# Other slots for the loads, splits and turns of q and k in a fused attention and MLP kernel

## The chip, the cores and the metric

The kernel runs on one core of one Trainium2 chip. The metric is the device time of one execution in microseconds (us). Before the change three executions took 505.07, 507.79 and 510.07 us, so the median is 507.79 us. One more execution was profiled.

Engines: PE multiplies matrices (PEld is its weight load), DVE is the vector engine, ACT the scalar engine, POOL is GpSimd, and SP is the sync engine, which here only issues DMAs.

## The reference, cut to what matters

```python
# q, k, v: (8 batches, 8 heads, 576 positions, 64), float32; w_in (512, 2048), w_out (2048, 512)
scores = scale * np.matmul(q, k.transpose(0, 1, 3, 2))
thresh = np.max(scores, axis=-1, keepdims=True) - tau        # tau = 0.02
scores = np.where(scores >= thresh, scores, -1000000000.0)
attn = softmax(scores)
attn_out = np.matmul(attn, v)
x = attn_out.transpose(0, 2, 1, 3).reshape(8 * 576, 512)
h = x @ w_in
out = (h - np.tanh(h)) @ w_out
```

An attention that keeps only scores within tau of the row's maximum is followed by a two-layer MLP over the 4608 tokens.

## The kernel before, in words

**Tiles.** Two heads of one batch form a pair; there are 32 pairs (NPAIR), and each has nine tiles of 128 query rows (TPP = 9), so 288 tiles in all. A tile's chain is: scores on PE (L387, matmuls L401 and L410), scaling and row maximum on DVE into sc (L420), a shift by maximum and tau on DVE (L432), the threshold on ACT into z (L447), the transpose of z into zT, exp on ACT into pT (L483, or L475 where PE made the transpose), and the product with v on PE (L506 to L524). From pair 6 on, zT is made by a DMA transpose on SP's queue, one for two tiles (L454).

**Preparing a pair.** k and q are loaded as float32 (kraw, qraw), split on POOL into a float16 high and low part (khl, qhl; three instructions, L228, L231, L232), and turned, so that the head dimension lies across partitions (kT, qT). In pairs 0 to 7 PE turns q, in pairs 0 to 8 it turns k; after that `turn` issues a DMA transpose on SP's queue (L315). A swapped copy of kT, kS, is made on POOL (`swap`, L337, two copies), after kT is there: the scores of a tile use kT and kS. v is copied to bf16 on POOL (`split_v`, L261 to L266). From pair 8 on, loads are issued by ACT's queue (`load_part`, L175) in up to two parts for each tensor. Raw tiles and split tiles have two buffers for each tensor (`raw_pool`, `hl_pool`), kT, qT and kS three each (`qk_pool`).

**Order.** The schedule is written out by hand: a loop over slots s, from -8 on (L852). In slot s the program emits, in this order, the shift of tile s + 7, the scores of tile s + 8, the threshold of tile s + 5 with its zT transpose when that tile is odd (so at even slots), tanh of the MLP, exp of tile s (from pair 6 on), MLP matmuls and their store, attention of tile s - 2, and last the planned steps of the slot (`plan`, L899). Each engine works through its own instructions in that order and waits only for semaphores; so a slot is a place in each queue and no fixed time.

**The plan.** The first scores of pair p stand in slot 9p - 8. A step with the number d stands d slots earlier, at 9p - 8 - d. The names in the table `LATER` (even pairs under 0, odd ones under 1) and in `FIRST_LATER` (pairs 8 and 9, which begin the scheme) are: k0, q0, q1, v0, v1 for the loads' parts; ks, qs, vs for splits; kt, qt for turns; kw for the swap. The loop at L784 puts them into `plan`. The parts are 288 KB for k, 256 and 32 KB for q, 160 and 128 KB for v.

Beside this, from pair 4 on, the MLP's matmuls are spread over the slots of four pairs at a time (hidden layer psH L579, second layer psY L605, a store of 256 KB for each 128 rows, L620), and after the last tile the rest of the MLP runs alone.

Of the kernel before, what the change touches and what calls it, by code (L numbers as in the profile page):

```python
# [18 lines left out]
def kernel(  # L19
# [713 lines left out]
    def w_load(piece):  # L733
# [6 lines left out]
        else:  # L740
# [18 lines left out]

    LATER = {  # L760
        0: (
            ("kt", 11), ("qt", 7), ("k0", 18), ("q0", 17), ("v0", 13),
            ("q1", 14), ("v1", 10), ("ks", 12), ("qs", 8), ("vs", 4),
            ("kw", 6),
        ),
        1: (
            ("kt", 10), ("qt", 6), ("k0", 18), ("q0", 14), ("v0", 15),
            ("q1", 13), ("v1", 12), ("ks", 11), ("qs", 8), ("vs", 6),
            ("kw", 5),
        ),  # L770
    }
    FIRST_LATER = {
# [3 lines left out]
            ("kw", 3),  # L776
        ),
        9: (
            ("kt", 10), ("qt", 6), ("k0", 18), ("q0", 14), ("v0", 15),
            ("q1", 13), ("v1", 12), ("ks", 11), ("qs", 8), ("vs", 6),  # L780
            ("kw", 5),
        ),
    }
    for p in range(DUAL, NPAIR):  # L784
# [176 lines left out]
```

## Time and profile before

| what | value |
|---|---|
| three executions, median | 507.79 us |
| the profiled execution | 511.62 us |
| its span | 509.7 us |
| PE busy | 484.8 us, 95% of the span |
| ACT busy | 431.7 us, 85% |
| DVE busy | 400.2 us, 79% |
| POOL busy | 291.4 us, 57% |
| DMA transposes zT, kT, qT | 117, 23, 24 |
| median from issue to landing: zT, kT, qT | 4.7, 5.2, 4.3 us |
| longest from issue to landing: zT, kT, qT | 9.8, 8.8, 6.3 us |

The profile is one execution. Busy time counts an engine's instructions; an instruction that only waits or issues a DMA is not counted. A queue name with a q, such as SPq or ACTq, is the issuing side of that engine. A line of waits has the form "who waited <- for whom: us in total, times, longest". A releaser is inferred from semaphores. The span splits in two: to about 440 us attention and MLP run together, and after that the remaining MLP runs alone. The granted TensorE clock was 0.57 on average between 104 and 108 us and full in the stretches around it.

### The profile page before, as it was taken

What the parts mean: (1) busy time and instruction counts of PE and PEld (TensorE: products, weight loads), DVE (VectorE), ACT (ScalarE), POOL (GpSimd) and SP (SyncE); (2) the same over time, 40 slices, a digit from 0 to 9 for tenths busy, and PEclk for the clock granted to TensorE, in tenths of its full rate; (3) what the DMA queues carried; (4) which work ended last, traced back from release to release, by engine and by line L of the source; (5) the groups of instructions that cost most, each with busy time, mean ns of one, the idle gap of its engine ahead of it and who ended that gap; (6) DMA issues with size and microseconds to landing.
All of it is one profiled execution on the core that took longest, in us unless ns stands there. A gap on an engine that the chain in (4) does not pass through costs nothing.

```text
span 509.7 us, 12184 instructions
## 1 busy us (share of the span) xinstructions
PE 484.8 (95%) x4283; PEld 270.9 (53%) x4345; DVE 400.2 (79%) x1150; ACT 431.7 (85%) x617; POOL 291.4 (57%) x390
## 2 busy tenths in 40 slices
PE   8999899889999989999999999999998999999997
PEld 4666566445555545555555555555554555544444
DVE  5899978878889879988898789889886887544440
ACT  5999998889999889999999999899979999533430
POOL 8999999886765375757675666569456700000000
PEclk9999999989999999999999999999999999999999
DMA  7852658999999999999999999999999986311013
GB/s 206 262 155 89 195 190 220 159 225 214 231 217 245 192 254 209 238 241 242 242 195 221 261 238 225 207 242 240 213 191 258 187 144 115 87 41 42 23 41 82
DMA packets 233341, 95.32 MB, mean 187 GB/s; under 512 B 203968, under 2 KB 222656, under 8 KB 233280
## 3 DMA queue, kind: packets, MB, share of 16 engines
q1 hardware_dynamic: 212336, 72.87, 75.1%
q10 hardware_dynamic: 20944, 21.67, 16.1%
q8 instruction: 34, 0.56, 0.5%
q14 instruction: 27, 0.22, 0.2%
HBM read 36.70 MB, written 9.44 MB: 91 GB/s over the span
## 4 chain that ended last, share of the span: by engine, by line
PE 57%; POOL 12%; DMA 9%; issue 7%; ACT 7%; DVE 5%; ACTq 1%; SPq 0%; POOLq 0%; DVEq 0%
PE psY L605 18%; PE psH L579 14%; PE psS L410 13%; DMA zT<-z 6%; PE psO L513 3%; POOL kS L337 3%; PE psHt L579 3%; ACT pT L483 3%; DMA vraw<-in_v_dram 3%; ACT z L447 2%; DVE g L598 2%; POOL qhl L232 2%; DVE sc L420 2%; PE psS L401 2%; ACTq L175 1%
## 5 line engine op out<-in xcount | busy, mean ns | idle before, releaser
L420 DVE TENSOR_SCALAR_CACHE_REDUCE sc<-psS 128x576 f32<-128x576 f32 x288 | 213.5, 752 | 27.1 <-PE psS L410 12.9
L447 ACT ACTIVATE z<-sc,nb 128x576 bf16<-128x576 f32 x288 | 216.1, 770 | 8.0 <-DVE nb L432 5.7
L483 ACT ACTIVATE pT<-zT 128x1152 f16<-128x1152 bf16 x117 | 135.2, 1155 | 12.3 <-DMA zT<-z 10.6
L605 PE MATMUL psY<-w_out_sb,g 128*128 128x512 bf16 (+1 forms) x564 | 140.8, 373 | 1.6 <-issue 0.2
L579 PE MATMUL psH<-xT,w_in_sb 128*128 128x512 bf16 x448 | 119.4, 381 | 5.1 <-issue 2.0
L337 POOL COPY kS<-kT 64x1152 f16<-64x1152 f16 x62 | 70.8, 1142 | 86.3 <-DMA kT<-khl 72.7
L598 DVE SCALAR_TENSOR_TENSOR g<-th,psH 128x512 bf16<-128x512 f32 x128 | 87.6, 685 | 33.6 <-ACT th L592 32.9
L410 PE MATMUL psS<-kT,qT 128*128 128x512 f16 (+1 forms) x512 | 104.7, 286 | 4.1 <-DVE sc L420 1.9
L410 PE MATMUL psS<-kS,qT 128*128 128x512 f16 (+1 forms) x512 | 105.1, 287 | 0.0
L410 PEld LDWEIGHTS <-qT 128*128 128x128 f16 x1024 | 72.5, 98 | 59.0 <-issue 3.8
L592 ACT ACTIVATE th<-psH 128x512 f32<-128x512 f32 x128 | 74.6, 583 | 21.4 <-PE psH L579 21.4
L605 PEld LDWEIGHTS <-g 128*128 128x128 bf16 x592 | 51.1, 98 | 54.6 <-DVE g L598 0.4
L579 PEld LDWEIGHTS <-w_in_sb 128*128 128x128 bf16 x576 | 49.4, 98 | 57.4 <-issue 6.3
L513 PE MATMUL psO<-vb,pT 128*128 128x65 bf16 x1024 | 53.3, 194 | 0.0
L513 PEld LDWEIGHTS <-pT 128*128 128x128 f16 x1024 | 44.2, 98 | 9.6
L232 POOL TENSOR_TENSOR qhl<-qraw,qhl 128x576 f16<-128x576 f32 x31 | 39.7, 1281 | 2.6
L232 POOL TENSOR_TENSOR khl<-kraw,khl 128x576 f16<-128x576 f32 x31 | 39.7, 1280 | 2.7
L475 ACT ACTIVATE pT<-psZ 128x512 f16<-128x512 bf16 (+1 forms) x54 | 35.1, 654 | 2.4 <-PE psZ L466 2.1
L506 PE MATMUL psO<-vb,pT 128*128 128x130 bf16 x128 | 28.2, 220 | 3.7 <-ACT pT L483 3.6
L617 DVE COPY yo<-psY 128x512 f32<-128x512 f32 (+1 forms) x31 | 21.1, 680 | 13.1 <-PE psY L605 12.4
L539 DVE TENSOR_TENSOR osb<-psO,rc 128x256 bf16<-128x256 f32 x64 | 27.2, 424 | 2.2
L228 POOL TENSOR_SCALAR qraw<-qraw 128x576 f32<-128x576 f32 x31 | 20.8, 671 | 11.1 <-DMA qraw<-in_q_dram 10.8
(77 smaller groups left out, 452.1 us busy)
## 6 DMA issues: line engine op xcount, KB each, us to landing
out_dram<-yo SPq DMA_DIRECT2D x32, 256.0 KB, 3.8
kraw<-in_k_dram ACTq DMA_DIRECT2D x24, 288.0 KB, 4.2
qraw<-in_q_dram ACTq DMA_DIRECT2D x24, 256.0 KB, 4.3
wt<-in_moe_w_in_dram SPq DMA_DIRECT2D x8, 512.0 KB, 4.6
wt<-in_moe_w_out_dram SPq DMA_DIRECT2D x8, 512.0 KB, 3.9
vraw<-in_v_dram ACTq DMA_DIRECT2D x24, 160.0 KB, 4.3
vraw<-in_v_dram ACTq DMA_DIRECT2D x24, 128.0 KB, 3.8
vraw<-in_v_dram SPq DMA_DIRECT2D x8, 256.0 KB, 3.6
```

What stands on the lines that cost most here:

```text
L232: nc.gpsimd.tensor_tensor(out=hl[:, :, 1, :], in0=x, in1=hl[:, :, 0, :], op=ALU.subtract)
L337: nc.gpsimd.tensor_copy(out=o, in_=i)
L410: nc.tensor.matmul(out=ps[:, dst], lhsT=lhs, rhs=cols(p, kk, hh), start=(n == 0), stop=(n == 1),)
L420: nc.vector.tensor_scalar(out=sc, in0=ps[:, lo : lo + S], scalar1=SC, scalar2=None, op0=ALU.mult, op1=ALU.max, accum_out=mx[:, c : c + 1],)
L447: nc.scalar.activation(out=z, in_=sc, func=ACT.Prelu, bias=nb, scale=1.0, alpha=STEEP)
L475: nc.scalar.activation(out=pt[:, off * P : (off + n) * P], in_=ps[:, 0 : n * P], func=ACT.Exp)
L483: nc.scalar.activation(out=pt[:, 0 : n * P], in_=zts.pop(i)[:, 0:n, :], func=ACT.Exp)
L513: nc.tensor.matmul(out=po[:, t - 1 + ab, :], lhsT=pt[:, blk * P : (blk + 1) * P], rhs=vb[:, hh, c, :], start=False, stop=(n == 7), skip_gr ...
L579: nc.tensor.matmul(out=ps, lhsT=w_in_sb[:, c, n * P : (n + 1) * P], rhs=xs[m][:, c, :] if m < B else xR[:, c, :, :], start=(c == 0), stop= ...
L592: nc.scalar.activation(out=th, in_=ps, func=ACT.Tanh)
L598: nc.vector.scalar_tensor_tensor(out=gs[m][:, n, :], in0=th, scalar=-1.0, in1=ps, op0=ALU.mult, op1=ALU.add,)
L605: nc.tensor.matmul(out=ps, lhsT=gs[m][:, n, ms * P : (ms + 1) * P], rhs=w_out_sb[:, n, cols], start=(n == 0), stop=(n == DF_C - 1),)
```

## The change

Only numbers d in the tables change; pair 8 keeps its own.

```diff
     LATER = {
         0: (
-            ("kt", 11), ("qt", 7), ("k0", 18), ("q0", 17), ("v0", 13),
-            ("q1", 14), ("v1", 10), ("ks", 12), ("qs", 8), ("vs", 4),
+            ("kt", 11), ("qt", 7), ("k0", 22), ("q0", 19), ("v0", 14),
+            ("q1", 17), ("v1", 13), ("ks", 14), ("qs", 10), ("vs", 4),
             ("kw", 6),
         ),
         1: (
-            ("kt", 10), ("qt", 6), ("k0", 18), ("q0", 14), ("v0", 15),
-            ("q1", 13), ("v1", 12), ("ks", 11), ("qs", 8), ("vs", 6),
-            ("kw", 5),
+            ("kt", 8), ("qt", 6), ("k0", 18), ("q0", 15), ("v0", 19),
+            ("q1", 14), ("v1", 11), ("ks", 11), ("qs", 9), ("vs", 6),
+            ("kw", 3),
         ),
     }
     FIRST_LATER = {
...
         9: (
-            ("kt", 10), ("qt", 6), ("k0", 18), ("q0", 14), ("v0", 15),
-            ("q1", 13), ("v1", 12), ("ks", 11), ("qs", 8), ("vs", 6),
-            ("kw", 5),
+            ("kt", 8), ("qt", 6), ("k0", 18), ("q0", 15), ("v0", 19),
+            ("q1", 14), ("v1", 11), ("ks", 11), ("qs", 9), ("vs", 6),
+            ("kw", 3),
         ),
     }
```

The plan repeats after two pairs, that is after 18 slots. Counted from the slot that is 18 before the first scores of an even pair (0), the steps stand at these places; zT transposes stand at 0, 2, 4, ... 16 in both.

| step | before | after |
|---|---|---|
| even pair: k0, q0, q1 | 0, 1, 4 | 14, 17, 1 |
| even pair: v0, v1 | 5, 8 | 4, 5 |
| even pair: k split, q split | 6, 10 | 4, 8 |
| even pair: k turn, q turn, swap, v split | 7, 11, 12, 14 | 7, 11, 12, 14 |
| odd pair: k0, q0, q1 | 9, 13, 14 | 9, 12, 13 |
| odd pair: v0, v1 | 12, 15 | 8, 16 |
| odd pair: k split, q split | 16, 1 | 16, 0 |
| odd pair: k turn, q turn | 17, 3 | 1, 3 |
| odd pair: swap, v split | 4, 3 | 6, 3 |

So every k or q split now stands three slots or more ahead of its turn (before, one to three), and the earliest load stands 22 slots ahead (before, 18).

## The prediction

> **What bounds the kernel now.** I read the 40 slices first. PE is at 9 tenths nearly throughout, and from the eighth slice to the 33rd the 16 DMA engines are at 8 or 9 tenths too:
>
> ```profile
> PE   8999899889999989999999999999998999999997
> ...
> DMA  7852658999999999999999999999999986311013
> ```
>
> The change acts only on loads, splits and turns of pairs 9 to 31, so next I read the busy time by stretches of 40 us where those run (columns: stretch and its us, PE, PEld, DVE, ACT and POOL busy us with counts, granted clock, DMA share, GB/s):
>
> ```profile
> 120.00:160.00 40.00, 39.58 (x350) 21.77 (x355) 34.95 (x104) 39.49 (x55) 27.18 (x36) 1.00 1.18 229
> 160.00:200.00 40.00, 38.24 (x337) 20.69 (x342) 32.87 (x98) 36.91 (x51) 24.80 (x30) 1.00 1.22 214
> 200.00:240.00 40.00, 39.58 (x353) 21.83 (x358) 35.88 (x107) 39.18 (x55) 27.15 (x36) 1.00 1.19 238
> ...
> 360.00:400.00 40.00, 37.64 (x331) 20.54 (x336) 33.78 (x101) 35.56 (x50) 23.47 (x31) 1.00 1.22 218
> ...
> sum 320.00, PE 311.83 PEld 170.88 DVE 272.79 ACT 302.91 POOL 185.41; mean PE 38.98 PEld 21.36 DVE 34.10 ACT 37.86 POOL 23.18
> ```
>
> A good stretch leaves PE 0.4 us of 40 unused, and ACT no more. From 120 to 440 us PE is idle for 320 - 311.83 = 8.2 us. The four good stretches leave 0.42 to 0.56 each, so about 8 x 0.5 = 4 us is floor and **4.2 us is all that a better order of transfers could win there**. Another 4 us lies before: PE gaps of 1.27, 0.77 and 1.55 us at 98.9, 102.0 and 104.0 us, the last one waiting for pair 8's qT, whose plan the change leaves alone.
>
> Then the waits:
>
> ```profile
> POOL kS L337 <- DMA kT<-khl: 72.7, 20, 7.9
> ...
> ACT pT L483 <- DMA zT<-z: 10.6, 11, 2.2
> ...
> PE psO L506 <- ACT pT L483: 3.6, 4, 1.3
> ...
> PE psS L401 <- POOL kS L337: 0.4, 1, 0.4
> ```
>
> The 72.7 us of POOL are large and cost nothing: POOL runs ahead of the slots and stands before the swap until kT has landed, and PE waited 0.4 us, once, early, for a kS. What reaches PE is a late zT: ACT waits for it, then PE for pT. The two that do it after 120 us are at 183.11 (0.34 us) and 383.85 (1.24 us, with 0.58 at 386.39 behind it). An instance of what makes transfers late is pair 21's kT, its issue in SP's timeline and the swap that waits for it in POOL's (start, us, engine and line, what, and the idle time before with its releaser):
>
> ```profile
> 264.18 2.59 SPq L315 DMA_TRANSPOSE kT<-khl  x1
> ```
>
> ```profile
> 272.46 2.33 POOL L337 COPY kS<-kT 64x1152 f16<-64x1152 f16 x2 [7.11 <-DMA kT<-khl]
> ```
>
> 8.3 us from issue to swap, where the median landing is 5.2. In ACT's timeline the k and first q loads of pair 22 (288 and 256 KB) are issued at 263.35 and 265.4, inside that flight. Pairs 17, 25 and 29 show 6.1, 8.2 and 7.8 us; the twelve odd pairs average 5.9.
>
> **What the Trainium skill says.** *DMA: Bandwidth & Descriptors*, section "Issuing engines are not separate DMA queues": DMAs of ScalarE and SyncE end on the same 16 engines and interleave. The trace agrees: between 120 and 400 us SP's queue q1 takes 94.5% and ACT's q10 24.7% of the 16 engines' time, over 100% together, so a load moved takes room from a transpose. *Perfetto Trace Analysis*, section "Tensor Engine Instruction (MATMUL, LD_WEIGHTS)": ACT, DVE and GpSimd are strictly first in, first out. It agrees above: POOL sat 7.11 us before kS with the next pair's k split (274.87) behind it. The same page, "Optimization Strategy": find the gaps of the engine to be optimized and what blocks it. That is the way taken here.
>
> **The change part by part.** No instruction is added or removed: 23 pairs keep their five loads (ACT's queue), two splits, one v split and one swap (POOL) and two transposes (SP); durations stay 0.34 to 0.61 us per load issue, 2.6 us per split (0.67 + 0.66 + 1.28), 2.33 per swap, 1.3 to 1.7 per transpose issue. Only positions move. A slot lasts (414.8 - 118.6)/198 = 1.50 us, from ACT's z at the first slots of pairs 9 and 31.
>
> *Splits two slots earlier for even pairs and one for odd q.* POOL, 58% busy in these stretches, runs ahead anyway: in the trace even k splits end 9.1 to 11.9 slots before the pair where 12 is written. It removes some of SP's waits for POOL at L315, about 36 us in 27 waits from 120 us on. But SP also waits 173 us there for ACT before a zT, so it has room; the waits only delay a zT queued behind, on average by 1.0 us at the slots after the odd turns. Worth 0 to 1 us; I take 0.5. If POOL were behind, it would be worth nothing.
>
> *Odd kT two slots later (10 to 8), odd swap two slots later (5 to 3).* This moves a transpose past one zT on SP's queue and past an even k split on POOL's. It takes 2 x 1.50 = 3.0 us from the cover between kS and its first use. I measured that cover in before, from the end of the second swap copy to the pair's first sc less 1.0 us for its matmuls: pairs 9, 11, ... 31 have 5.4, 7.1, 5.6, 5.5, 2.8, 5.5, 2.1, 4.2, 2.1, 7.0, 4.4, 8.0 us. Less 3.0, pairs 17, 21 and 25 come out 0.2, 0.9 and 0.9 short, **2.0 us of PE waiting if kT takes as long as now**. But the loads that lengthened these very flights are moved (next), so I take 0.5; bounds 0 to 9, the upper end under the rivals.
>
> *Loads.* In the 18-slot cycle the even k and q0 leave slots 0 and 1, where odd kT flew, for 14 and 17: 544 KB go out of slots 0 to 4 and kT comes in. Slots 0 to 4 then hold five transposes in a row (zT, kT, zT, qT, zT), where slots 17 to 4 held five over six slots. At 1.3 to 2.0 us to issue each, 5 slots of 1.50 us are just filled, so the zT of slot 4 goes out some 0.5 us later. Its cover: from issue to pT is 6.4 us on average, landing 4.7, so 1.7 us. Mostly hidden; in 11 cycles it costs 0 to 3 us, taken as 1. The gain: the late-zT groups near 270 to 273 and 378 to 383 us lie in flights like pair 21's; the latter cost PE 1.24 + 0.58. I take 1.7 won. The groups near 174 to 182 and 285 lie behind even kT, whose slot 7 keeps a v load and the odd k load close by: nothing won there.
>
> *Buffers.* A load waits in ACT's order for POOL to have read the tile two pairs back. Tightest are pair 9's v, now issued at the end of slot 54 (about 88.7 us), with pair 7's v split done at 85.2, and pair 10's k at slot 60 (about 99), its reader done at 92.7. Both are covered by 3.5 us or more; should POOL lag that much, ACT stops with z and pT behind it.
>
> *Start.* Pair 10's k (288 KB) comes at 99 instead of 104 us, into the flight of pair 8's qT (97.6 to 104), which PE already waits 1.55 us for; pair 9's q leaves it. Behind that gap the granted clock was 0.57 from 104 to 108 us, (1 - 0.57) x 4 = 1.7 us more, which may go or stay with the gap. Between -3 and +2 us; I take +0.5.
>
> Sum: -0.5 + 0.5 + 1.0 - 1.7 + 0.5 = -0.2 us, none to speak of. The profiled execution took 511.62 us (span 509.7 and 1.9 around it), 3.8 above the median of 507.79, so **about 508 us** for a median.
>
> **Rivals.** *Faster:* the even loads were what made flights long; odd kT falls from 5.9 to about 4.5 us, ACT no longer waits for zT, and all 4.2 us above the floor go, with 1.5 from the start. 511.6 - 5.7 is 505.9, on the median's scale 502. For it: the collision in pair 21. Against: even turns keep their neighbours, and four of the eight stretches have nothing to give. *Slower:* five transposes in a row lengthen odd kT, and PE stops before each such pair's first scores for kS. With 1 us more of flight than in before, pairs 17, 21 and 25 cost 1.2 + 1.9 + 1.9 = 5.0 us; with 2 us, 2.2 + 2.9 + 0.8 + 2.9 + 0.6 = 9.4. It decides from 1 us on, and gives 513 to 517. For it: transposes are what fills the queue (94.5%); DMA has no spare time to even out into. Against: 544 KB leave. *It does nothing:* POOL's run-ahead means that splits happen when their loads land, not where they are written; then 508 too, within the first case.
>
> **How the numbers follow.** Within 1% (502.7 to 512.9), about what a measurement of this kernel can tell from no change given runs of 505 to 510: 0.53. Slower by more, through the kS or through a late zT on ACT: 0.32. Faster by more, which needs over half of every PE gap there is: 0.15. The range goes from the faster case to the 9.4 us of the slower, 502 to 517.
>
> **What would show it.** Right: odd kT to kS at 5 us or less, no line of PE waiting for kS, SP's waits for POOL at L315 mostly gone, PE idle between 120 and 440 us still 6 to 9 us. Wrong towards slower: psS or sc waiting for L337, ACT's wait for zT above 15 us. Wrong towards faster: that idle time at 5 us or below. A wait of a load for POOL on ACT's queue near 88 us would break the part on buffers.

## The result, and the profile after

The changed kernel took **516.63 us** (median of 14 executions, 511.12 to 523.71) beside 508.37 us for the kernel before (14 executions, 504.61 to 516.24): a ratio of **1.0162, interval 1.0128 to 1.0195**, so 8.3 us slower. Every ratio here and below leaves out the executions that took over 1.5% longer than the fastest of their kernel, so it can differ from the ratio of the medians. The profiled execution of the changed kernel took 515.12 us, with a span of 513.3.

The slices of the page, PE and the 16 DMA engines:

```profile
PE   8999899889999999999999999989999999999996
...
DMA  7852658999999999999999999999999976311013
```

Nothing is to be seen there: PE still shows nines, and DMA is as full and as even as it was. The stretches of 40 us show it (columns as before the change: PE, PEld, DVE, ACT, POOL, granted clock, DMA share, GB/s):

```profile
200.00:240.00 40.00, 38.15 (x325) 20.57 (x329) 33.50 (x99) 37.55 (x53) 27.47 (x37) 1.00 1.21 227
...
280.00:320.00 40.00, 38.67 (x339) 21.12 (x344) 33.85 (x100) 36.89 (x51) 27.08 (x36) 1.00 1.16 226
320.00:360.00 40.00, 36.19 (x303) 19.15 (x306) 30.82 (x93) 34.20 (x47) 21.97 (x28) 0.96 1.25 198
...
sum 320.00, PE 308.74 PEld 168.13 DVE 268.69 ACT 298.60 POOL 185.98; mean PE 38.59 PEld 21.02 DVE 33.59 ACT 37.33 POOL 23.25
```

PE's idle time from 120 to 440 us went from 8.2 to 320 - 308.74 = 11.3 us. Two stretches that had been good lost 1.4 and 0.8 us (200 and 280), and the worst one, at 320, leaves 3.8 us idle. The sum tells more than the single stretches: e4 below is the same program as before under other numbers, and in its profile the stretch at 280 lost 1.9 us while the sum is 8.4. The waits between 120 and 440 us:

```profile
POOL kS L337 <- DMA kT<-khl: 53.1, 17, 5.2
...
ACT pT L483 <- DMA zT<-z: 14.3, 16, 3.9
...
PE psO L506 <- ACT pT L483: 2.4, 1, 2.4
PE psS L401 <- DMA qT<-qhl: 1.9, 2, 1.0
```

PE never waits for a kS. ACT's wait for zT, 8.8 us in these stretches before, is 14.3, and PE now waits twice for a qT.

A stage clock is better than windows that cut different work: from the start of ACT's 82nd z (first tile of pair 9) to its 280th (pair 31), the trace gives **297.6 us before and 303.5 after, 5.9 us more**. The 82nd z itself started 2.7 us earlier (122.7 and 120.0 us), and so the span grew by 3.6 only. Those 2.7 us are not the change's: e4 has that z at 119.2, and so have all others but e2 (119.2 to 120.9; e2 123.6). The profiles of before and e2 both show three gaps of PE, of 0.8 to 1.9 us each, between 97 and 106 us, and a granted clock of 0.50 for 3.4 us from 104 us on; why only some executions have them was not tried.

### The profile page after: what moved, and what is told of

Same layout as the page of the kernel before. It is cut to its first block, busy times and chain, and to the rows that moved or that the text cites. A ratio compares the mean times of both kernels' runs of the same rounds, so it can differ in the third digit from the quotient of the medians.

```text
span 513.3 us, 12187 instructions
## 1 busy us (share of the span) xinstructions
PE 486.2 (95%) x4283; PEld 271.0 (53%) x4345; DVE 399.3 (78%) x1150; ACT 432.1 (84%) x617; POOL 292.0 (57%) x390
## 3 DMA queue, kind: packets, MB, share of 16 engines
q10 hardware_dynamic: 20944, 21.67, 17.2%
## 4 chain that ended last, share of the span: by engine, by line
PE 65%; POOL 9%; DMA 9%; ACT 6%; DVE 5%; issue 5%; ACTq 0%; SPq 0%; POOLq 0%; DVEq 0%
PE psY L605 20%; PE psH L579 16%; PE psS L410 15%; DMA zT<-z 5%; PE psO L513 4%; PE psHt L579 3%; ACT z L447 3%; PE psS L401 2%; DMA qT<-qhl 2%; DVE g L598 2%; DVE sc L420 2%; ACT pT L483 2%; ACT th L592 1%; PE psO L524 1%; POOL qhl L232 1%
## 5 line engine op out<-in xcount | busy, mean ns | idle before, releaser
L420 DVE TENSOR_SCALAR_CACHE_REDUCE sc<-psS 128x576 f32<-128x576 f32 x288 | 213.4, 751 | 31.9 <-PE psS L410 17.2
L483 ACT ACTIVATE pT<-zT 128x1152 f16<-128x1152 bf16 x117 | 135.2, 1155 | 15.2 <-DMA zT<-z 14.9
L579 PE MATMUL psH<-xT,w_in_sb 128*128 128x512 bf16 x448 | 119.2, 380 | 4.4 <-issue 1.7
L261 POOL CAST vb<-vraw 128x512 bf16<-128x512 f32 x32 | 19.7, 617 | 9.8 <-PE psS L410 4.6
```

The source lines that it names most:

```text
L420: nc.vector.tensor_scalar(out=sc, in0=ps[:, lo : lo + S], scalar1=SC, scalar2=None, op0=ALU.mult, op1=ALU.max, accum_out=mx[:, c : c + 1],)
L483: nc.scalar.activation(out=pt[:, 0 : n * P], in_=zts.pop(i)[:, 0:n, :], func=ACT.Exp)
L579: nc.tensor.matmul(out=ps, lhsT=w_in_sb[:, c, n * P : (n + 1) * P], rhs=xs[m][:, c, :] if m < B else xR[:, c, :, :], start=(c == 0), stop= ...
```

## Where the trace shows the loss

The collision that the prediction described is gone. Pair 21's kT, 8.3 us from issue to swap before, takes 3.9: SP's issue and POOL's swap in the changed kernel (start, us, engine and line, what, idle time before with its releaser):

```profile
266.53 2.06 SPq L315 DMA_TRANSPOSE kT<-khl  x1
```

```profile
270.44 2.32 POOL L337 COPY kS<-kT 64x1152 f16<-64x1152 f16 x2 [1.91 <-DMA kT<-khl]
```

All odd kT fly 4.3 us on average (5.9 before), and each kS is ready 1.3 to 5.6 us before its first use. What grew is the time from the end of a z to its zT. I split it into the lag (from the end of the second z to SP's issue) and the flight (issue to landing), for the 103 zT of slots 66 to 270, by place in the 18-slot cycle; means in us:

| place | 0 | 2 | 4 | 6 | 8 | 10 | 12 | 14 | 16 |
|---|---|---|---|---|---|---|---|---|---|
| lag before | 0.62 | 0.44 | 0.86 | 0.46 | 1.11 | 0.77 | 1.19 | 0.40 | 0.11 |
| lag after | 0.03 | 0.78 | 1.08 | 1.16 | 1.57 | 1.08 | 1.77 | 0.35 | 0.19 |
| flight before | 5.21 | 4.48 | 4.20 | 4.96 | 5.13 | 5.03 | 5.31 | 4.98 | 5.34 |
| flight after | 4.54 | 4.52 | 4.57 | 5.05 | 5.42 | 5.65 | 5.01 | 5.25 | 5.85 |

With kT moved from place 17 to place 1, the zT of place 0 gains 0.6 us, and every one from 2 to 12 loses 0.2 to 0.7: the lags sum to 92.6 us instead of 68.3. This is the moved turn's mark: in the four kernels with the odd kT at place 1 (the change, e1, e5, e12) the lags sum to 93 to 123 us, in the four with it at place 17 (before, e2, e3, e4) to 68 to 82; those with transposes added or exp moved are left out.

A zT with lag and flight over 8 us, which is about what the five slots between z and exp leave, came 5 times before, in five different places, and 8 times after, all at places 8, 10 and 12. The count alone says little, since e4, the same program as before, has 9, in seven places. The worst one after the change, in the timelines of SP, ACT and PE:

```profile
330.51 1.30 SPq L454 DMA_TRANSPOSE zT<-z  x1
331.92 1.69 SPq L315 DMA_TRANSPOSE kT<-khl  x1
333.70 5.20 SPq L454 DMA_TRANSPOSE zT<-z  x2
339.01 3.27 SPq L315 DMA_TRANSPOSE qT<-qhl  x1
```

```profile
342.68 1.16 ACT L483 ACTIVATE pT<-zT 128x1152 f16<-128x1152 bf16 x1 [3.88 <-DMA zT<-z]
```

```profile
343.89 0.23 PE L506 MATMUL psO<-vb,pT 128*128 128x130 bf16 x1 [2.45 <-ACT pT L483]
```

SP issues one transpose after another with pauses of 0.1 us, the two zT take 5.2 us to issue, ACT stands 3.88 us for a zT, and PE 2.45 us for the pT behind it. In windows of 2 us the DMA engines move little from 336 to 342 us, and then PE stops and its granted clock falls:

```profile
336.00:338.00 2.00, 2.00 (x25) 1.17 (x23) 1.98 (x8) 2.00 (x3) 0.55 (x1) 1.00 1.95 139
338.00:340.00 2.00, 1.95 (x21) 1.17 (x21) 1.50 (x5) 0.79 (x2) 1.89 (x3) 1.00 0.70 107
340.00:342.00 2.00, 1.45 (x9) 0.48 (x7) 2.00 (x6) 0.00 (x0) 1.74 (x5) 1.00 1.36 118
342.00:344.00 2.00, 0.11 (x3) 0.11 (x4) 0.56 (x3) 1.32 (x2) 1.91 (x2) 1.00 1.18 265
344.00:346.00 2.00, 2.00 (x17) 0.94 (x17) 0.77 (x2) 2.00 (x3) 0.00 (x0) 0.69 1.11 250
```

**Such a stop can cost twice.** Behind the 2.45 us gap the clock was 0.50 for 3.4 us, worth 0.50 x 3.4 = 1.7 us; the stage of before has no such stretch. With the 3.1 us by which PE's idle time grew, that makes 4.8 of the stage's 5.9 us. The other executions point the same way: the granted clock averages 0.9938 over the change's 14, and 0.9989 to 0.9992 over those of the kernel before that were run beside the experiments (27 to 43 each). As an estimate from these means, that is 3.2 us of lost clock against 0.4 to 0.6. The clocks of before in the change's own batch are not on record, so how much of the 8.3 us this makes is not shown.

The slumps of the transfer rate are not the change's: of the 148 windows of 2 us from 122 to 418 us, 17 lie under 120 GB/s in before and 14 in after.

## The experiments

The theories. **Queue:** the turn at place 1 pushes later zT back on SP's queue. **Loads:** the new places of the loads lengthen flights around the even turn. **Order on POOL:** a split that stands behind a swap makes SP wait. In one table, each against the kernel before that was run with it (median 508.3 to 509.1 us); stage and ACT's wait for zT (120 to 440 us) are from the one profiled execution:

| run | ratio | interval | stage, us | wait for zT, us |
|---|---|---|---|---|
| before | 1 | | 297.6 | 8.8 |
| the change | 1.0162 | 1.0128 to 1.0195 | 303.5 | 14.3 |
| e1 turns only | 1.0183 | 1.0108 to 1.0259 | 310.7 | 23.4 |
| e2 turns back | 1.0100 | 1.0030 to 1.0171 | 303.2 | 17.2 |
| e3 loads only | 1.0055 | 1.0011 to 1.0100 | 297.8 | 9.8 |
| e4 splits only | 1.0047 | 1.0021 to 1.0074 | 299.0 | 12.3 |
| e5 turns and k split | 1.0065 | 1.0033 to 1.0096 | 305.8 | 18.9 |
| e6 extra transposes, place 1 | 1.0197 | 1.0097 to 1.0297 | 304.2 | 16.5 |
| e7 extra transposes, place 15 | 1.0315 | 1.0236 to 1.0393 | 314.1 | 24.5 |
| e8 k turn earlier | 1.0182 | 1.0123 to 1.0241 | 305.7 | 18.0 |
| e9 before, two slots more | 1.0078 | 1.0052 to 1.0104 | 296.8 | none |
| e10 after, two slots more | 1.0106 | 1.0075 to 1.0137 | 300.1 | none |
| e11 as e7, two slots more | 1.0340 | 1.0281 to 1.0400 | 314.1 | none |
| e12 after, odd v back | 1.0058 | 1.0024 to 1.0093 | 302.6 | 16.4 |

The profiled executions of e1, e2 and e5 were 3.7 to 4.6 us above their kernels' medians, and e6's was 8.9 below; in these four the ratio decides, not the stage. Before and e4 are one program, and their stages differ by 1.4 us and their waits by 3.5; smaller differences in these two columns say nothing.

**e1: the odd turn and swap alone.** The tables of before, with kt and kw changed (the same under 9):

```diff
         1: (
-            ("kt", 10), ("qt", 6), ("k0", 18), ("q0", 14), ("v0", 15),
+            ("kt", 8), ("qt", 6), ("k0", 18), ("q0", 14), ("v0", 15),
...
-            ("kw", 5),
+            ("kw", 3),
```

> Only the odd pairs' k turn (10 to 8) and swap (5 to 3) are moved; loads and splits stay as before. Turn theory (the 8 us come from five transposes in a row, kT, zT, qT, zT, which send the odd qT and the zT behind it late): ratio to before 1.012 to 1.02, PE waiting for qT in odd pairs, as in the changed kernel (1.0 us each at 115, 331 and 390 us there). Load theory (the 8 us come from the even k and q loads crowding places 14 to 17): ratio 0.995 to 1.005. Both parts needed: 1.003 to 1.01. With the old loads still in the flight of kT, a long kT (8 us) may also leave PE waiting for kS.

1.0183: the moved turn without the moved splits costs as much as the whole change. Part of that is not the turn itself. POOL's timeline:

```profile
277.33 2.33 POOL L337 COPY kS<-kT 64x1152 f16<-64x1152 f16 x2 [4.21 <-DMA kT<-khl]
279.75 0.68 POOL L228 TENSOR_SCALAR kraw<-kraw 128x576 f32<-128x576 f32 x1
280.49 0.66 POOL L231 CAST khl<-kraw 128x576 f16<-128x576 f32 x1
281.24 1.28 POOL L232 TENSOR_TENSOR khl<-kraw,khl 128x576 f16<-128x576 f32 x1
```

and SP's:

```profile
280.21 1.58 SPq L454 DMA_TRANSPOSE zT<-z  x1
282.55 2.68 SPq L315 DMA_TRANSPOSE kT<-khl  x1
285.32 6.82 SPq L454 DMA_TRANSPOSE zT<-z  x2
```

POOL stands 4.21 us before the odd swap, now with the even k split behind it. The split ends at 282.52, and SP, free at 281.79, issues the even kT only at 282.55. Over all even kT that makes 12.8 us of gaps on SP, up to 1.8 each; about 0.1 us stands before every DMA, and the rest is for this split (before: 2.5 in all). The zT behind it come late, and PE waits for the pT made from them:

```profile
PE psO L506 <- ACT pT L483: 8.4, 3, 3.1
```

**e2: the change with the odd turn and swap back.**

```diff
-            ("kt", 8), ("qt", 6), ("k0", 18), ("q0", 15), ("v0", 19),
+            ("kt", 10), ("qt", 6), ("k0", 18), ("q0", 15), ("v0", 19),
...
-            ("kw", 3),
+            ("kw", 5),
```

> The changed kernel with the odd k turn and swap back at 10 and 5; new loads and splits stay. Turn theory: back to before, ratio 0.995 to 1.003, no wait of PE for qT. Load theory: it stays at 1.012 to 1.02, with late zT at ACT (14 us in the changed kernel, 10.6 before).

1.0100, between what the two theories forecast: some of the loss goes with the turn, by the ratios 0.6%, but the intervals of the two overlap.

**e3: the loads alone.** The tables of before with k0, q0, v0, q1, v1 of the change; splits, turns and swaps as before.

```diff
-            ("kt", 11), ("qt", 7), ("k0", 18), ("q0", 17), ("v0", 13),
-            ("q1", 14), ("v1", 10), ("ks", 12), ("qs", 8), ("vs", 4),
+            ("kt", 11), ("qt", 7), ("k0", 22), ("q0", 19), ("v0", 14),
+            ("q1", 17), ("v1", 13), ("ks", 12), ("qs", 8), ("vs", 4),
...
-            ("kt", 10), ("qt", 6), ("k0", 18), ("q0", 14), ("v0", 15),
-            ("q1", 13), ("v1", 12), ("ks", 11), ("qs", 8), ("vs", 6),
+            ("kt", 10), ("qt", 6), ("k0", 18), ("q0", 15), ("v0", 19),
+            ("q1", 14), ("v1", 11), ("ks", 11), ("qs", 8), ("vs", 6),
```

> Only the loads are moved as in the change. Load theory: 1.012 to 1.02. Turn theory: 0.995 to 1.003, perhaps a little faster since the odd kT flies without the even k and q loads (5.9 us on average before, 4.3 in the changed kernel).

1.0055, with a stage of 297.8 us: no gain from the loads, a small loss at most. Their zT fly 5.4 and 5.7 us at places 8 and 10, as in the change (5.4 and 5.65) and longer than in before (5.1 and 5.0). But they fly 5.5 us at both in e4, where no load moved, so this is not shown to come from the loads.

**e4: the splits alone.**

```diff
-            ("q1", 14), ("v1", 10), ("ks", 12), ("qs", 8), ("vs", 4),
+            ("q1", 14), ("v1", 10), ("ks", 14), ("qs", 10), ("vs", 4),
...
-            ("q1", 13), ("v1", 12), ("ks", 11), ("qs", 8), ("vs", 6),
+            ("q1", 13), ("v1", 12), ("ks", 11), ("qs", 9), ("vs", 6),
```

> Only the splits are moved: even k 12 to 14, even q 8 to 10, odd q 8 to 9. All theories so far: 0.997 to 1.003, since POOL runs ahead of the slots anyway. If it is slower, POOL's order is a cause by itself: splits queued before the swap.

1.0047, and this is the measure of everything else: on every engine the instructions stand in the same order and wait for the same as in the kernel before, because no split passes another POOL step. **A kernel that is the same came out 0.5% slower with an interval that leaves out 1.** So a difference of 0.5% between two builds is not read as an effect here. All thirteen ratios of the table lie above 1; should every build beside before carry this half percent, the change's own loss is nearer 1.1% (1.0162 / 1.0047). Whether it is chance or common to all was not tried.

**e5: e1 with the even k split moved out of the way.**

```diff
-            ("q1", 14), ("v1", 10), ("ks", 12), ("qs", 8), ("vs", 4),
+            ("q1", 14), ("v1", 10), ("ks", 14), ("qs", 8), ("vs", 4),
...
-            ("kt", 10), ("qt", 6), ("k0", 18), ("q0", 14), ("v0", 15),
+            ("kt", 8), ("qt", 6), ("k0", 18), ("q0", 14), ("v0", 15),
...
-            ("kw", 5),
+            ("kw", 3),
```

> The odd k turn and swap moved as in the change (10 to 8, 5 to 3), and the even k split at 14, so that POOL makes it ahead of the odd swap; loads stay as before. In the run with the turns alone SP stood 12.8 us before the even kT for this split, which stood in POOL's queue behind the swap. Chain theory (that wait was its whole loss): back to 1.000 to 1.005. Queue theory (kT moved into the half of the cycle in which SP's queue is full, so zT behind it go out late): 1.006 to 1.015, with SP's wait for the split gone (under 3 us) and SP's total lag behind z (68 us before, 123 with the turns alone) between 80 and 100 us.

The gaps before the even kT fall from 12.8 to 1.2 us, and the ratio from 1.0183 to 1.0065. So the order on POOL carries over half of e1's loss; the change does not have it, since it moves this split too. What is left for the turn is 0.65%, hardly more than e4's 0.47%, although SP's lags sum to 116 us here, more than in the change.

**e6 and e7: a price for one more transpose.** A transpose of a blank tile into a spare one that nobody reads, once in each odd pair from 9 on (12 in all), at place 1 in e6 and at place 15 (with 12 for 8) in e7. It tests whether the queue has slack near the odd turn's place in before that it lacks near its new one.

```diff
+    blank = const.tile([P, W], FP16, name="blank")
+    spare = const.tile([P, W], FP16, name="spare")
+    nc.vector.memset(blank, 0.0)
+    def extra():
+        nc.sync.dma_start_transpose(
+            out=spare.rearrange("p (c r) -> p c r", c=TPP), in_=blank
+        )
+    for p in range(9, NPAIR, 2):
+        plan.setdefault(TPP * p - AHEAD - 8, []).append(extra)
```

> The kernel before with twelve extra DMA transposes of the size of kT, from a blank tile to a spare one, at place 1 of the cycle, where the change puts the odd kT; nothing waits for them. Queue theory: each pushes the following zT back, 1.006 to 1.015, with later zT at places 4 to 12. If only the cover of kS or POOL's order counts, 0.998 to 1.004.

> The same twelve extra transposes at place 15, in the half of the cycle with few turns. Queue theory: less than at place 1, 1.000 to 1.005. If it is the sheer number of transposes on the DMA engines that counts and not the place, as much as at place 1.

The theory of a slack half fell: place 15 costs no less than place 1. The ratios say 1.97% at place 1 and 3.15% at place 15, but their intervals overlap, and by the medians of all executions both lose 3.0 to 3.3% (524.33 and 526.01 us beside 509.13), so a difference between the places is not shown. Of 509 us this is 10 to 17 us, so 0.8 to 1.4 us for each, though nothing waits for their data. In e7 they surface as late zT:

```profile
PE psO L506 <- ACT pT L483: 9.7, 6, 2.5
```

**e8: the odd k split and turn two slots earlier**, the other way from the change.

```diff
-            ("kt", 10), ("qt", 6), ("k0", 18), ("q0", 14), ("v0", 15),
-            ("q1", 13), ("v1", 12), ("ks", 11), ("qs", 8), ("vs", 6),
+            ("kt", 12), ("qt", 6), ("k0", 18), ("q0", 14), ("v0", 15),
+            ("q1", 13), ("v1", 12), ("ks", 13), ("qs", 8), ("vs", 6),
```

> The other way: the kernel before with the odd k turn at 12 and its split at 13, one zT earlier on SP's queue. Queue theory: SP's queue is freer at place 0, lag no larger than before, ratio 0.995 to 1.002; a gain would be small since before leaves PE 4.2 us above its floor. If before sits at a narrow optimum for another reason, slower, 1.003 or more.

1.0182, with the smallest sum of lags of all (62.8 us). SP had to wait up to 2.8 us for the k split at this turn (4.9 us in all), and the zT of place 16 then lagged 1.6 us and flew 6.1. So the queue theory's forecast failed, though the late split stands beside the moved turn as a second cause. The sum of lags does not decide; six zT of place 16 came later than 8 us.

**e9, e10, e11: two more slots between z and exp.** From pair 6 on, exp, attention and the MLP stand two slots later; z and zT stay, so every zT has seven slots to land instead of five. Done to before (e9), to the change (e10) and to e7 (e11):

```diff
-    SOONER = (4, 4, 4, 4, 0, 0, 0)
+    SOONER = (4, 4, 4, 4, 0, 0, -2)
...
-    for s in range(-AHEAD, NTILE + LAG + 3):
+    for s in range(-AHEAD, NTILE + LAG + 5):
...
-        if 0 <= s < NTILE and j == 2 + LAG and p % HPAIR == 0 and p >= HPAIR:
+        if 0 <= s < NTILE and j == 4 + LAG and p % HPAIR == 0 and p >= HPAIR:
...
-            todo = [(s + n, step) for n, step in enumerate(layers(stage, True))]
+            todo += [(s + 2 + n, step) for n, step in enumerate(layers(stage, True))]
```

> The kernel before, with exp, attention and the MLP's steps two slots later in the stretch where zT comes by DMA (from pair 6 on), so that a zT has seven slots instead of five between z and exp. Budget theory (before and all changes so far lose by zT that need more than the five slots, some 8 us from the end of z): ACT's wait for zT after 120 us falls from 8.8 us to under 3, and the time by 3 to 8 us less the longer pipeline at the end: ratio 0.985 to 1.0. If late zT only show where PE is held up by something else, 1.0 to 1.01.

> The changed kernel with the same two slots more. Budget theory: its loss against before goes, within 0.5% of the run of before with two slots more. If the change's loss comes from late qT or kT instead (PE waited 1.9 us for qT in it), at least 1% above that run.

> The kernel with twelve extra transposes at place 15 (1.0315), with the same two slots more. Budget theory: most of its loss goes, within 1% of the run of before with two slots more, since the extra transposes cost PE nothing but through late zT. If the DMA engines as such are the bound, it stays 2 to 3% above it.

ACT's wait for zT before exp is gone in all three. In e9 whole stretches then show no idle time on PE, in part because its trace is fuller (in the stage 709 matmuls of the MLP are on record, in before's 666):

```profile
200.00:240.00 40.00, 40.00 (x359) 21.93 (x358) 35.72 (x105) 39.26 (x54) 27.19 (x36) 1.00 1.18 239
...
280.00:320.00 40.00, 40.00 (x357) 21.78 (x356) 35.86 (x104) 38.72 (x54) 27.20 (x36) 1.00 1.19 232
```

Its stage is the shortest of all, 296.8 us, yet the time is 0.8% longer: the two slots mostly come back as a later end (from the 280th z to the last instruction 92.8 us instead of 89.5), and a few qT are late. Between e9 and e10 the ratios leave 1.0106 / 1.0078 = 1.003 of the change's 1.016, but with such intervals that is 0.999 to 1.007. The medians of all executions (511.25 and 515.70 us) leave 4.45 of its 8.3 us, and the stages 3.3 of 5.9. **So the late zT carry between about half and most of the loss; that they carry all of it is not shown.** In e11 the loss stays (1.034), and the wait list names what PE waits for instead:

```profile
PE psS L401 <- DMA qT<-qhl: 8.2, 6, 2.4
...
PE psH L579 <- DVE g L598: 6.0, 5, 3.3
```

SP's lags sum to 295 us there, 157 in e9: with the extra transposes the queue falls further behind, and with a longer lead for zT a late qT is the next thing to wait for.

**e12: the change with the odd v load back at place 12.**

```diff
-            ("kt", 8), ("qt", 6), ("k0", 18), ("q0", 15), ("v0", 19),
+            ("kt", 8), ("qt", 6), ("k0", 18), ("q0", 15), ("v0", 15),
```

> The changed kernel with one load moved back: the odd pair's v0 (160 KB) at place 12 again instead of place 8, where it flies beside the even kT (7), zT (8) and the odd k0 (9). That this load is what lengthened the zT flights of places 8 and 10: flights there go back to 5.0 to 5.4 us (5.4 and 5.65 in the changed kernel), ACT's wait for zT between 120 and 440 us falls below 12 us (14.3), ratio to the kernel before 1.008 to 1.012. That another load (the even k0, q0 and q1, the odd q) or the moved odd turn carries the loss: 1.014 to 1.018, the wait stays above 13 us, flights at 8 and 10 above 5.4 us.

The time says yes and the trace no. The ratio of 1.0058 is a percent below the change's, twice what e4 shows for no difference; by the medians (513.84 beside 508.91 us) it is 0.65% below. But in its profile the flights at places 8 and 10 are 5.35 and 6.2 us, 17 zT take over 8 us, and ACT waits longer, not shorter:

```profile
ACT pT L483 <- DMA zT<-z: 16.4, 16, 2.5
```

So moving this load probably wins back some of the loss, but not by the way that I expected; one profile is too little to say how. No version ran faster than the kernel before.

## Why the prediction was right and wrong

The 516.6 us lie inside the range, at the end that belongs to the slower rival (513 to 517), and the likeliest case of 508 was missed by 8.6. That the range holds them is luck in part: its upper end is a sum of PE's stops for kS, and there was none. What bounded the kernel was read rightly: PE, with late transposes behind its longest stops. But PE's idle time, forecast at 6 to 9 us from 120 to 440 us, came to 11.3. By its steps:

- **Splits, -0.5: wrong, 0.** The step took 36 us of SP's waits at L315 from the list of waits. The timeline of before shows that SP stood idle before its 46 turns for 6.8 us in all, 0.6 at most, about 0.1 of it before every DMA anyway: 34 of the 36 us are time in which SP was already issuing that very transpose. The same list still had 27.0 us after the change, where "mostly gone" was forecast, while the gaps came to 5.4. The 173 us before zT, from which the step took that SP has room, were misread in the same way: the timeline from 120 to 440 us has 43 us of idle time before zT. The 1.0 us of lag that the step put behind the odd turns (places 0 and 4 of the table: 0.62 and 0.86) is larger behind the even ones (8 and 12: 1.11 and 1.19), which did not move.
- **kS, +0.5: right in kind, 0.** No wait for kS; odd kT flies 4.3 us, where "5 or less" was the sign. That rival's main mechanism, PE stopping for kS, did not occur.
- **Later zT, +1.0 for the zT of slot 4: this term failed.** The five transposes in a row were seen, and of the 0.5 us at place 4 some came (0.2). But the backlog does not end there. It runs on to place 12, over the even turns, where the lag was already the largest. With mean flight and mean cover (1.7 us) a tail of late zT can't be seen, and the clock behind a stop of PE had no price in this term. ACT's wait for zT rose by 5.5 us in these stretches, and the stage by 5.9, 1.7 of it by the clock; e10 shows that late zT are about half of the loss or more.
- **Loads, -1.7: not won.** The flights of odd kT shortened as said, by the loads alone to 5.2 us in e3 (5.9 in before, 6.2 in e4), which agrees with what the Trainium skill says (*DMA: Bandwidth & Descriptors*, section "Issuing engines are not separate DMA queues"): loads and transposes run on the same DMA engines. But e3 is no faster than before. Whether the loads took that room from other transposes is not shown (e3 above).
- **Buffers: right.** ACT issued pair 9's first v load at 87.1 us without waiting for POOL.
- **Start, +0.5: nothing.** The 82nd z came 2.7 us earlier, but so it does in e4, which changes nothing.
- **POOL's order.** The step said that the odd swap passes an even k split, and gave that no price. It costs nothing in the change because the split moves as well; e1 shows what it was worth, about 1.2% by e1 against e5.
- **The rival** named "a late zT on ACT" as its second way, and that is the one. Its sign in the profile, more than 15 us of ACT's wait, was just missed with 14.9 on the whole page.

What stays open: how the 1.6% divides. Turn with k split (e5, 0.65%) and loads (e3, 0.55%) each come out near what a kernel without any difference shows (0.47%), and only both together lose clearly more. That the two need each other is the likeliest reading, but the intervals do not settle it. Which load matters is not settled either; e12 points weakly at the odd v. The part of the loss that e10 leaves, and why the transfer rate slumps now and then, were not tried.

## What to carry to other kernels

On a queue that is nearly always issuing, a transfer moved to another place is paid by all those behind it up to the next gap; look up which of them has the least cover, and look at the latest ones, not at the mean. Price a long stop of the bounding engine with the clock behind it. Read a queue's waits from its timeline, since a list of waits can count time in which the queue was busy. And measure and profile one version that changes nothing: here it sets 0.5% as the least that can be called an effect, and shows that the number of late zT differs as much between two profiles of one program (5 and 9) as between before and the change (5 and 8).

## What the runs showed of the hardware

- A DMA transpose that nothing waits for cost 0.8 to 1.4 us of the kernel's time (e6, e7), about what SP needs to issue one (1.2 us and up), in a stage where SP's queue takes 94.5% of the 16 engines' time (before, 120 to 400 us).
- The granted clock was 0.50 for 3.4 us behind some stops of PE: after gaps of 2.45 us in the change, 2.73 and 3.09 in e1, 2.30 and 3.27 in e11. It stayed full after 2.58 us in e1, 2.55 in e7 and 2.38 in e11, so the length of the gap alone does not decide.
- Two zT transposes issued together took 5.2 us in the change and 6.82 us in e1 to leave SP. From 336 to 342 us DMA moved 107 to 139 GB/s in the change, and from 284 to 290 us less still in e1, where about 220 is the mean:

```profile
284.00:286.00 2.00, 2.00 (x14) 0.94 (x11) 2.00 (x6) 1.77 (x4) 1.25 (x1) 1.00 1.69 99
286.00:288.00 2.00, 2.00 (x24) 1.21 (x22) 1.98 (x7) 0.00 (x0) 0.00 (x0) 1.00 0.82 72
288.00:290.00 2.00, 0.68 (x5) 0.22 (x3) 0.93 (x4) 0.00 (x0) 0.00 (x0) 1.00 1.31 103
```

The slumps come in every kernel here, 8 to 18 windows of 148, and do not go with the loss: e7, one of the slowest, has 8.
